# New ranks for the opening of a fused attention and feed-forward kernel, one rounding moved from GpSimd to ScalarE, and one subtraction placed beside another stage

## The chip, the cores and the metric

The kernel runs on one core of one Trainium2 chip. The metric is the device time of one execution in microseconds; a median of several runs is given. A core has five engines with queues of their own, which run in order: TensorE (PE, matrix products), VectorE (DVE), ScalarE (ACT), GpSimd (POOL), and SyncE (SP), which issues the DMA transfers here. PE reads its operands from SBUF and writes to PSUM[...].

## The reference

```python
q, k, v: (4, 4, 1088, 32);  S1, S2: (8, 32) float64;  w1, w2: (128, 1024), w3: (1024, 1024), w_out: (1024, 128) float64

def phi(x):                                   # 64 features from 32 numbers
    a = np.einsum('rd,bhsd->bhsr', S1, x)
    b = np.einsum('rd,bhsd->bhsr', S2, x)
    return np.einsum('bhsi,bhsj->bhsij', a, b).reshape(*x.shape[:-1], 64)
q_p, k_p = phi(q), phi(k)
kv = np.einsum('bhsf,bhsd->bhfd', k_p, v)
z = np.sum(k_p, axis=2)
num = np.einsum('bhsf,bhfd->bhsd', q_p, kv)
den = np.einsum('bhsf,bhf->bhs', q_p, z)[..., None] + 1e-06
x = (num / den).transpose(0, 2, 1, 3).reshape(4352, 128)
out = ((x @ w1) * (x @ w2) @ w3) @ w_out      # (4352, 128)
```

The denominator can come close to zero, so it needs more than float32's precision in the products that lead to it. The kernel gets this by splitting numbers into a leading part, rounded to a coarse grid, and a rest.

## The kernel before

**Stages.** The 4 batches of 1088 rows are cut into 9 groups: two of 512 columns for each batch (groups 0 to 7) and one of 256 columns with the remaining 64 rows of every batch (group 8). For each batch b there is a *key stage*: keys are split (`peak`, `first`, `second`), their Gram matrix is summed on PE (`gs0`, `gs1`, and `rg` for the remaining 64 rows of each batch), and a chain of small steps takes it through the sketches S1 and S2 to the matrix R, from which the denominators follow: `G_lead`, `G_rest`, `T_mm`, `T_lead`, `T_rest`, `N_mm`, `N_lead`, `N_rest`, alternately on DVE and PE. Beside it the key features `kp` are formed and summed against v (`k_ab`, `b_copy`, `kp`, `kv`, and `r_tr` to `rv` for the remaining rows). For each group there is a *query stage*: `tr` (transpose on DVE), `grid` (row maximum to a rounding constant), `lead` (two ACT instructions that give the rounded query q1), `rem` (POOL adds: the rest q2 of the query), `ay1` and `ay2` (PE products with R), `split`, `dens`, `dens2`, `phi` on DVE, then transposes and `nd` on PE and a copy that gives xT. Then the *feed-forward stage* of the group: for each of 8 chunks c `a` and `b` on PE (two products each), `a_copy` on ACT, `mul` on DVE, and `o` on PE with w3·w_out, which is formed once in the kernel (`w3_t`, `w3_t_copy`, `w3_mm`). The float64 weights come as raw words and are converted on ACT (`words`) and DVE (`conv`).

**Order.** No queue's order is written out by hand. Every step is entered into a `Plan` with an engine, an estimated duration, what it reads and writes, and a rank. `Plan.order()` simulates the five queues: for each engine it takes, among the steps that could start within 0.1 us of the earliest, the one with the lowest rank; a step of much lower rank (by over 0.9) that becomes ready within 0.35 us (`FIRST["wait"]`) is waited for. Tiles with few buffers are handed out in the order of entry. The instructions are issued in the order that results, and each engine keeps it. The steps of the opening have ranks from the table `EARLY` (-10 where it has no entry, -9 for the first query), those of the later stages from `FIRST`. `HELD` names the DVE steps that the planner takes to be slowed by POOL: 0.7 of the overlap is added to their duration.

**The opening.** `first_ops()` enters batch 0's key stage; `q_ops(0)` and `q_ops(1)` the queries of the first two groups. Groups 0 to 2 are "lean": `ay1` and `ay2` are separate steps. `first_rest` and `second_rest` split the remaining 64 rows of the keys of two batches (`kkr`): for batch 0 on POOL, with an add and a subtract of the constant for each half of the rows. Where the planner sees a gap of PE over 0.5 us before the first `o`, the kernel fills it with products on zeros (`idle`), on top of 14 of them at the very start:

```python
            if spare and t - busy > 0.5:
                idle(int((t - busy - 0.2) / 0.187))
```

The weight loads after the first two wait for a memset of one element on DVE, which is issued when the planner has passed `G_rest`.

Of the kernel before, what the change touches and what calls it, by code (L numbers as in the profile page):

```python
# [11 lines left out]
F32 = mybir.dt.float32  # L12
# [7 lines left out]
ACT = mybir.ActivationFunctionType  # L20
# [7 lines left out]
def bview(t, free):  # L28
# [12 lines left out]
MOST = 120  # L41
TURN = 0.1

FIRST = {"words": 1, "conv": 1.5, "early": 1.5, "k": 2, "KX": 10, "q": 0.8, "q_act": 1, "k_act": 0, "a": 2, "b": 2.1,
         "o": 0.9, "many": 6, "late": 3, "w3_t": 1, "w3_t_copy": 0, "w3_mm": 1.7, "k1": 1.3, "mul": 0.55, "wait": 0.35}

EARLY = {"tr": -9, "Pg": -8, "sT": -10, "grid": -8, "split": -10, "grid1": -2, "tr1": -7, "rem": -8.5, "rem1": -6,
         "lead": -10, "lead1": -6, "R": -7, "k_ab0": -11, "k_ab1": -6, "r_ab": -9, "r_tr": -9, "kv0": -12, "kv1": -5,
         "rv": -10, "P_mm": -12, "P_copy": -8, "P": -8, "kp0": -8, "kp1": -10, "r_kp": -8.5, "peak1": -8.5, "gs1": -12,
         "k_tr": -10, "rg": -11, "second_r": -9.5}  # L50

HELD = {"dens", "dens2", "conv", "second", "T_rest"}
LATENCY = {"PE": 0.27, "DVE": 0.2, "ACT": 0.23, "POOL": 0.3, "SP": 3.8}


class Plan:
# [36 lines left out]
    def order(self):  # L93
        ops = self.ops
        tiles = {tag: list(keys) for tag, keys in self.held.items()}
        end, left, res, clock = {}, [], [], {}
        columns = 128
        issued = []
        pool, held = [], (0.0, 0.0)
        turn = {}  # L100
        for op in ops:
            for key in op[5]:
                if key[0] not in SHARED:
                    turn.setdefault(key[0], []).append(key)
        for n, (_, engine, us, *_r) in enumerate(ops):
            if engine is None:
                end[n] = (None, us)
            else:
                left.append(n)

        def seen(n, engine):
            e, t = end[n]
            return t if e in (None, engine) and e != "SP" else t + LATENCY[e]

        while left:
            best = {}
            for i in left:
                _, engine, us, _, deps, new, rank = ops[i]
                if any(d not in end for d in deps):
                    continue  # L120
                t = max([clock.get(engine, 0.0)] + [seen(d, engine) for d in deps])
                ok = all(key[0] in SHARED or turn[key[0]][0] == key for key in new)
                for key in new:
                    before = tiles.get(key[0], [])
                    if len(before) >= BUFS[key[0]]:
                        users = self.users[before[-BUFS[key[0]]]]
                        if any(u not in end for u in users):
                            ok = False
                            break
                        t = max([t] + [seen(u, engine) for u in users])  # L130
                if engine == "PE" and COLUMNS.get(ops[i][0], 128) != columns:
# [22 lines left out]
            left.remove(i)  # L154
# [22 lines left out]
def kernel(  # L177
# [20 lines left out]
    nc = tc.nc  # L198
# [251 lines left out]
    def round_to(dst, src, g, engine=nc.vector):  # L450
        engine.tensor_scalar(dst, src, g, g, ALU.add, ALU.subtract)
# [237 lines left out]
    def rest_rows(m):  # L689

        for i in range(2):
            rows = slice(i * SR, (i + 1) * SR)
            yield k_rs[m][rows], kk_rs[rows, i], rows

    def first_rest(m, g, engine):
        for x, t, rows in rest_rows(m):
            if engine is nc.vector:
                round_to(t[:, 0], x, g[rows])
                continue
            gb = bview(g[rows], [[0, H], [0, D]])  # L700
            engine.tensor_add(t[:, 0], x, gb)
            engine.tensor_sub(t[:, 0], t[:, 0], gb)

    def second_rest(m, engine):
        for x, t, _ in rest_rows(m):
# [2 lines left out]
    def lead_first():  # L708

        g = {}  # L710

        def peak(n):
            g[n] = row_max(k_sb[0] if n == 0 else k_rs[0], 128, f"k{n}")

        def peaks():
            nc.vector.tensor_tensor(g[0], g[0], g[1], ALU.max)
            to_grid(g[0], 8)
            k_lead[0] = work.tile([128, 2, H, NJ, D], F32, tag="kk", bufs=1, name="kk")

        def first():  # L720
            round_to(k_lead[0][:, 0], k_sb[0], g[0])

        def second(part):
            t = k_lead[0]
            nc.vector.tensor_sub(part(t[:, 1]), part(k_sb[0]), part(t[:, 0]))
        chunks = lambda half: lambda t: t[:, :, 4 * half:4 * half + 4]
        return {"peak0": lambda: peak(0), "peak1": lambda: peak(1), "peaks": peaks,
                "first": first, "second0": lambda: second(chunks(0)), "second1": lambda: second(chunks(1)),
                "first_r": lambda: first_rest(0, g[0], nc.gpsimd), "second_r": lambda: second_rest(0, nc.gpsimd)}

    def lead(b):

# [447 lines left out]
    def q_ops(g):  # L1180
# [21 lines left out]
                p.op("load", "SP", 1.6, lambda: load_by_head("q", b + 2), (), (("qh", b + 2),), 3)  # L1202
        op("grid", "DVE", 0.35 + 0.6 * w, (qT,), (("gq", g),), after=begin)
        op("lead", "ACT", 0.2 + 1.2 * w, (qT, ("gq", g)), (("q1", g), ("q2", g)))
        op("rem", "POOL", 1.15, (qT, ("q1", g), ("q2", g)), (("q2", g),))
        R = [*(("R", b) for b in batches), *(("Rs", n) for n in range(4))]
        if lean:
            op("ay1", "PE", 0.25, (("q1", g), *(R if g else (("Rh", 0), ("Rs", 0)))), (("wa", "ay", g),), after=last_phi)
# [119 lines left out]
    def first_ops():  # L1328
# [19 lines left out]
        op("first", "DVE", 0.73, "first", (("k", 0), ("gk", 0)), (("kk", 0),))  # L1348
        op("second0", "DVE", 0.62, "second0", (("k", 0), ("kk", 0)), (("k2", 0),))
        op("second1", "DVE", 0.65, "second1", (("k", 0), ("kk", 0)), (("k2", 1),))  # L1350
        op("first_r", "POOL", 1.7, "first_r", (("kr", 0), ("gk", 0)), (("kkr", 0),))
        op("second_r", "POOL", 0.95, "second_r", (("kr", 0), ("kkr", 0)), (("kkr", 0),))
# [20 lines left out]
        op("P", "POOL", 1.93, sketch_P, (("Pc",), ("Pg",)), (("P",),))  # L1373
        op("T_lead", "DVE", 0.9, "T_lead", (("t", "T"),), (("Tp", 0),))
# [99 lines left out]
```

## Time and profile before

| what | us |
|---|---|
| median of 13 runs (276.28 to 278.57) | 277.52 |
| the profiled execution, its own time | 277.34 |
| its span, first to last instruction | 275.3 |
| PE busy (share of the span) | 268.2 (97%) |
| DVE busy | 209.1 (76%) |
| ACT busy | 122.7 (45%) |
| POOL busy | 21.3 (8%) |
| products on zeros, L358: 55 instructions | 14.8 |

The profile is of one execution. Its timeline gives for each row the start in us from the span's start, the duration, engine, line, operation, out <- in with the shape, and in brackets the idle time before it with what ended it. Rows of the same kind that follow one another are merged, with their count. A second view gives busy time by stretch of the span, a third the chain of work that ended last. Busy PE time holds the products on zeros too. The granted clock of PE is 1.000 of full speed in the mean.

### The profile page before, as it was taken

What the parts mean: (1) busy time and instruction counts of PE and PEld (TensorE: products, weight loads), DVE (VectorE), ACT (ScalarE), POOL (GpSimd) and SP (SyncE); (2) the same over time, 40 slices, a digit from 0 to 9 for tenths busy, and PEclk for the clock granted to TensorE, in tenths of its full rate; (3) what the DMA queues carried; (4) which work ended last, traced back from release to release, by engine and by line L of the source; (5) the groups of instructions that cost most, each with busy time, mean ns of one, the idle gap of its engine ahead of it and who ended that gap; (6) DMA issues with size and microseconds to landing.
All of it is one profiled execution on the core that took longest, in us unless ns stands there. A gap on an engine that the chain in (4) does not pass through costs nothing.

```text
span 275.3 us, 6300 instructions
## 1 busy us (share of the span) xinstructions
PE 268.2 (97%) x2556; PEld 150.8 (55%) x2556; DVE 209.1 (76%) x507; ACT 122.7 (45%) x265; POOL 21.3 (8%) x31
## 2 busy tenths in 40 slices
PE   7989999999999999999999999999999999999995
PEld 3766544477774767745544446455544544444665
DVE  7889999999999999996648699847695585583231
ACT  4693796997775992111332240224123222323120
POOL 2772000100000010000010010001000100000000
PEclk9999999999999999999999999999999999999999
DMA  4739999579930220020200200020002002000203
GB/s 128 280 93 298 256 381 271 157 206 291 257 120 2 76 85 2 2 39 2 38 2 0 37 4 5 0 39 2 0 0 41 0 2 38 2 0 10 31 0 57
DMA packets 28876, 22.42 MB, mean 81 GB/s; under 512 B 20016, under 2 KB 25392, under 8 KB 28848
## 3 DMA queue, kind: packets, MB, share of 16 engines
q1 hardware_dynamic: 28704, 21.96, 29.2%
q8 instruction: 20, 0.33, 0.5%
q14 instruction: 8, 0.07, 0.1%
q10 hardware_dynamic: 144, 0.07, 0.1%
HBM read 19.80 MB, written 2.23 MB: 80 GB/s over the span
## 4 chain that ended last, share of the span: by engine, by line
PE 89%; DVE 7%; ACT 2%; issue 1%; DVEq 0%; ACTq 0%
PE ps_o L1292 21%; PE b_ps L1273 20%; PE a_ps L1263 20%; PE ps_w3o L577 5%; PE ps_kvz L775 4%; PE ps_wt L565 3%; PE idle_ps L358 3%; PE ps_c L1034 2%; PE ps_o L1288 1%; PE ps_xt L1156 1%; PE ps_ab L672 1%; DVE ab L1278 1%; DVE ph L1109 1%; PE ps_c L1047 1%; PE ps_c L1045 1%
## 5 line engine op out<-in xcount | busy, mean ns | idle before, releaser
L1268 ACT COPY ffa<-a_ps 128x512 f32<-128x512 f32 (+1 forms) x72 | 40.4, 562 | 104.1 <-PE a_ps L1263 103.4
L1278 DVE TENSOR_TENSOR ab<-ffa,b_ps 128x512 f32<-128x512 f32 (+1 forms) x72 | 46.6, 650 | 41.1 <-PE b_ps L1273 38.3
L1273 PE MATMUL b_ps<-xT,w 128*128 128x512 f32 (+1 forms) x144 | 71.1, 575 | 0.0
L1263 PE MATMUL a_ps<-xT,w 128*128 128x512 f32 (+1 forms) x144 | 70.6, 572 | 0.1
L1292 PE MATMUL ps_o<-ab,w3o 128*128 128x512 f32 x128 | 65.7, 605 | 0.0
L1273 PEld LDWEIGHTS b_ps<-xT,w 128*128 128x128 f32 x144 | 26.2, 190 | 29.1 <-issue 24.3
L1263 PEld LDWEIGHTS a_ps<-xT,w 128*128 128x128 f32 x144 | 26.3, 190 | 27.2 <-issue 19.8
L1292 PEld LDWEIGHTS ps_o<-ab,w3o 128*128 128x128 f32 x128 | 22.8, 190 | 21.3 <-issue 18.8
L1007 POOL TENSOR_TENSOR q<-qT,q 128x512 f32<-128x512 f32 x8 | 9.6, 1196 | 184.1 <-ACT q L1003 180.6
L375 ACT CAST sgn<-cv_c 128x512 f16<-128x512 f32 x22 | 17.0, 773 | 0.0
L358 PE MATMUL idle_ps<-zeros 128*128 128x448 bf16 x55 | 14.8, 418 | 1.8 <-DVE zeros L352 1.8
L577 PE MATMUL ps_w3o<-wo,w3T 128*128 128x128 f32 x128 | 15.8, 275 | 0.5 <-issue 0.5
L577 PEld LDWEIGHTS ps_w3o<-wo,w3T 128*128 128x128 f32 x128 | 15.1, 192 | 1.1 <-issue 0.8
L411 ACT ACTIVATE cv_c<-raw 128x512 f32<-128x512 f32 x22 | 15.2, 689 | 0.0
L414 ACT ACTIVATE cv_m<-raw 128x512 int32<-128x512 uint32 x22 | 15.0, 682 | 0.0
L424 DVE CUSTOM_DVE_ANT_0 w3c<-w3c,cv_m 128x1024 uint16<-128x1024 uint16 x16 | 11.9, 742 | 0.4
L1109 DVE TENSOR_TENSOR ph<-ay,bs 128x512 f32<-128x512 f32 (+1 forms) x12 | 11.1, 947 | 0.2
L421 DVE SCALAR_TENSOR_TENSOR w3c<-cv_c,sgn 128x512 int32<-128x512 int32 x16 | 10.9, 684 | 0.3 <-ACT sgn L375 0.3
L565 PEld LDWEIGHTS ps_wt<-ident,w3c 128*128 128x128 f32 x64 | 7.7, 144 | 6.0 <-issue 2.8
L358 PEld LDWEIGHTS <-zeros 128*128 128x128 bf16 x55 | 5.9, 113 | 8.2 <-issue 3.8
L572 ACT COPY w3T<-ps_wt 128x512 f32<-128x512 f32 x16 | 9.4, 588 | 2.1 <-PE ps_wt L565 1.8
L565 PE MATMUL ps_wt<-ident,w3c 128*128 128x128 f32 x64 | 9.8, 276 | 0.0
(213 smaller groups left out, 355.1 us busy)
## 6 DMA issues: line engine op xcount, KB each, us to landing
raw<-in_moe_w_dram SPq DMA_DIRECT2D x20, 512.0 KB, 6.4
qh<-in_q_dram SPq DMA_DIRECT2D x4, 544.0 KB, 7.1
out_dram<-oT SPq DMA_DIRECT2D x33, 64.0 KB, 2.0
k_sb<-in_k_dram SPq DMA_DIRECT2D x4, 512.0 KB, 9.4
kh<-in_k_dram SPq DMA_DIRECT2D x12, 128.0 KB, 3.8
v_sb<-in_v_dram SPq DMA_DIRECT2D x12, 128.0 KB, 7.0
raw<-in_moe_w_out_dram SPq DMA_DIRECT2D x2, 512.0 KB, 6.8
v_sb<-in_v_dram SPq DMA_DIRECT2D x1, 512.0 KB, 5.3
```

The costliest lines, as they stand in the source:

```text
L358: nc.tensor.matmul(ps[:, :448], zeros[:, :128], zeros, start=True, stop=True)
L375: nc.scalar.copy(bview(t.bitcast(F16)[:, 1:], [[2, n]]), c)
L411: nc.scalar.mul(x["c"], halves(raw[n], CW)[1].bitcast(F32), 2.0 ** -112)
L414: nc.scalar.mul(x["m"].bitcast(I32), halves(raw.pop(n), CW)[0].bitcast(U32), 2.0 ** -29)
L565: nc.tensor.transpose(ps[i][:, c], w3c[i][:, c * 128:(c + 1) * 128], ident)
L577: nc.tensor.matmul(ps["mm"], w3T[ko][:, c], wo[:, c], start=(c == 0), stop=(c == NC - 1))
L1109: nc.vector.tensor_mul(ph[:, j:j + step].rearrange("p j h a b -> p (j h) a b"), bview(a, [[r, step * H], [1, r], [0, r]]), bview(b, [[r, s ...
L1263: nc.tensor.matmul(a_sb[g, c, "ps"][:, :n], w1[:, c * 128:(c + 1) * 128], xT[key], start=True, stop=True)
L1268: nc.scalar.copy(a_sb[g, c][:, :n], a_sb.pop((g, c, "ps"))[:, :n])
L1273: nc.tensor.matmul(ab_sb[g, c, "ps"][:, :n], w2[:, c * 128:(c + 1) * 128], xT[key], start=True, stop=True)
L1278: nc.vector.tensor_mul(ab_sb[g, c][:, :n], a_sb.pop((g, c))[:, :n], ab_sb.pop((g, c, "ps"))[:, :n])
L1292: nc.tensor.matmul(o_ps[g][:, :n], w3o[:, c], ab_sb.pop((g, c))[:, :n], start=c == 0, stop=c == NC - 1)
```

## The change

It has three parts.

1. `first_rest` for batch 0 runs on ACT: a `[128,1]` product by -1 that gives the negative constant, and then for each half of the rows one activation with the constant as bias, and one with its negative. `second_rest` stays on POOL.
2. In group 1, `rem` is entered behind `ay1` and depends on it; before it followed `lead`.
3. The tables change: `EARLY` gets new ranks for most steps of the opening (the Gram products, `P_mm`, `k_tr` and `first_r` have the lowest; `k_ab`, `kp`, `kv` and the remaining keys' steps the highest), `FIRST` has other ranks for `b`, `o` and `w3_t_copy`, `HELD` has three more names, and some estimated durations differ. The planner's search keeps a set of the steps whose inputs are planned, with the same rule of choice.

```diff
-FIRST = {..., "k_act": 0, "a": 2, "b": 2.1,
-         "o": 0.9, "many": 6, "late": 3, "w3_t": 1, "w3_t_copy": 0, "w3_mm": 1.7, ...}
-EARLY = {"tr": -9, "Pg": -8, "sT": -10, "grid": -8, "split": -10, "grid1": -2, "tr1": -7, "rem": -8.5, "rem1": -6,
-         "lead": -10, "lead1": -6, "R": -7, "k_ab0": -11, "k_ab1": -6, "r_ab": -9, "r_tr": -9, "kv0": -12, "kv1": -5,
-         "rv": -10, "P_mm": -12, "P_copy": -8, "P": -8, "kp0": -8, "kp1": -10, "r_kp": -8.5, "peak1": -8.5, "gs1": -12,
-         "k_tr": -10, "rg": -11, "second_r": -9.5}
-HELD = {"dens", "dens2", "conv", "second", "T_rest"}
+FIRST = {..., "k_act": 0, "a": 2, "b": 1.9,
+         "o": 1.95, "many": 6, "late": 3, "w3_t": 1, "w3_t_copy": 0.3, "w3_mm": 1.7, ...}
+EARLY = {"first_r": -13, "k_tr_copy": -12.5, "tr": -9, "Pg": -9.5, "sT": -9.2, "grid": -8, "split": -10, "grid1": -7,
+         "tr1": -7.5, "rem": -11, "rem1": -4.5, "lead": -11, "lead1": -8, "R": -7, "k_ab0": -6, "k_ab1": -5.9, "r_ab": -5.5,
+         "r_tr": -5.6, "kv0": -5, "kv1": -5, "rv": -5, "P_mm": -12, "P_copy": -9.5, "P": -12, "kp0": -5, "kp1": -5,
+         "r_kp": -4.6, "peak1": -9.5, "gs1": -12, "k_tr": -12, "rg": -11.5, "second_r": -12, "gs0": -12, "b_copy": -9,
+         "ay2": -10, "ay1": -11}
+HELD = {"dens", "dens2", "conv", "second", "T_rest", "phi", "second0", "second1"}
...
     def first_rest(m, g, engine):
+        if engine is nc.scalar:
+            minus = work.tile([128, 1], F32, tag="g_minus", bufs=1, name="g_minus")
+            engine.mul(minus, g, -1.0)
+            for grid, first in ((g, True), (minus, False)):
+                for x, t, rows in rest_rows(m):
+                    engine.activation(t[:, 0], x if first else t[:, 0], ACT.Identity, bias=grid[rows])
+            return
         for x, t, rows in rest_rows(m):
-            if engine is nc.vector:
-                round_to(t[:, 0], x, g[rows])
-                continue
-            gb = bview(g[rows], [[0, H], [0, D]])
-            engine.tensor_add(t[:, 0], x, gb)
-            engine.tensor_sub(t[:, 0], t[:, 0], gb)
+            round_to(t[:, 0], x, g[rows])
...
-                "first_r": lambda: first_rest(0, g[0], nc.gpsimd), ...
+                "first_r": lambda: first_rest(0, g[0], nc.scalar), ...
...
-        op("rem", "POOL", 1.15, (qT, ("q1", g), ("q2", g)), (("q2", g),))
+        def rem(after=()):
+            op("rem", "POOL", 1.15, (qT, ("q1", g), ("q2", g)), (("q2", g),), after=after)
+        if g != 1:
+            rem()
...
-            op("ay1", "PE", 0.25, ...)
+            ay1 = op("ay1", "PE", 0.25, ...)
+            if g == 1:
+                rem((ay1,))
...
-        op("first_r", "POOL", 1.7, "first_r", (("kr", 0), ("gk", 0)), (("kkr", 0),))
-        op("second_r", "POOL", 0.95, ...)
+        op("first_r", "ACT", 1.3, "first_r", (("kr", 0), ("gk", 0)), (("kkr", 0),))
+        op("second_r", "POOL", 1.0, ...)
-        op("P", "POOL", 1.93, ...)
-        op("T_lead", "DVE", 0.9, ...)
+        op("P", "POOL", 1.95, ...)
+        op("T_lead", "DVE", 0.7, ...)
```

More of the change, by code (lines that the diff above doesn't have):

```diff
@@ L42 @@
 TURN = 0.1
-FIRST = {"words": 1, "conv": 1.5, "early": 1.5, "k": 2, "KX": 10, "q": 0.8, "q_act": 1, "k_act": 0, "a": 2, "b": 2.1,
-         "o": 0.9, "many": 6, "late": 3, "w3_t": 1, "w3_t_copy": 0, "w3_mm": 1.7, "k1": 1.3, "mul": 0.55, "wait": 0.35}
-EARLY = {"tr": -9, "Pg": -8, "sT": -10, "grid": -8, "split": -10, "grid1": -2, "tr1": -7, "rem": -8.5, "rem1": -6,
-         "lead": -10, "lead1": -6, "R": -7, "k_ab0": -11, "k_ab1": -6, "r_ab": -9, "r_tr": -9, "kv0": -12, "kv1": -5,
-         "rv": -10, "P_mm": -12, "P_copy": -8, "P": -8, "kp0": -8, "kp1": -10, "r_kp": -8.5, "peak1": -8.5, "gs1": -12,
-         "k_tr": -10, "rg": -11, "second_r": -9.5}
-HELD = {"dens", "dens2", "conv", "second", "T_rest"}
+FIRST = {"words": 1, "conv": 1.5, "early": 1.5, "k": 2, "KX": 10, "q": 0.8, "q_act": 1, "k_act": 0, "a": 2, "b": 1.9,
+         "o": 1.95, "many": 6, "late": 3, "w3_t": 1, "w3_t_copy": 0.3, "w3_mm": 1.7, "k1": 1.3, "mul": 0.55, "wait": 0.35}
+EARLY = {"first_r": -13, "k_tr_copy": -12.5, "tr": -9, "Pg": -9.5, "sT": -9.2, "grid": -8, "split": -10, "grid1": -7,
[4 rows of a table added]
+HELD = {"dens", "dens2", "conv", "second", "T_rest", "phi", "second0", "second1"}
 LATENCY = {"PE": 0.27, "DVE": 0.2, "ACT": 0.23, "POOL": 0.3, "SP": 3.8}
@@ L113, in seen @@
             return t if e in (None, engine) and e != "SP" else t + LATENCY[e]
-        while left:
+        behind, open_deps, ready = {}, {}, set()
+        for n in left:
+            deps = [d for d in ops[n][4] if d not in end]
+            open_deps[n] = len(deps)
+            if not deps:
+                ready.add(n)
+            for d in deps:
+                behind.setdefault(d, []).append(n)
+        while ready:
             best = {}
-            for i in left:
+            for i in ready:
                 _, engine, us, _, deps, new, rank = ops[i]
-                if any(d not in end for d in deps):
-                    continue
                 t = max([clock.get(engine, 0.0)] + [seen(d, engine) for d in deps])
@@ L153, in order @@
             t, i, engine = first
-            left.remove(i)
+            ready.remove(i)
+            for n in behind.get(i, ()):
+                open_deps[n] -= 1
+                if not open_deps[n]:
+                    ready.add(n)
             us = ops[i][2]
@@ L695, in first_rest @@
     def first_rest(m, g, engine):
-        for x, t, rows in rest_rows(m):
-            if engine is nc.vector:
-                round_to(t[:, 0], x, g[rows])
-                continue
-            gb = bview(g[rows], [[0, H], [0, D]])
-            engine.tensor_add(t[:, 0], x, gb)
-            engine.tensor_sub(t[:, 0], t[:, 0], gb)
+        if engine is nc.scalar:
[5 more added lines that the diff above has]
+            return
+        for x, t, rows in rest_rows(m):
+            round_to(t[:, 0], x, g[rows])
     def second_rest(m, engine):
@@ L728, in lead_first @@
                 "first": first, "second0": lambda: second(chunks(0)), "second1": lambda: second(chunks(1)),
-                "first_r": lambda: first_rest(0, g[0], nc.gpsimd), "second_r": lambda: second_rest(0, nc.gpsimd)}
+                "first_r": lambda: first_rest(0, g[0], nc.scalar), "second_r": lambda: second_rest(0, nc.gpsimd)}
     def lead(b):
@@ L1204, in q_ops @@
         op("lead", "ACT", 0.2 + 1.2 * w, (qT, ("gq", g)), (("q1", g), ("q2", g)))
-        op("rem", "POOL", 1.15, (qT, ("q1", g), ("q2", g)), (("q2", g),))
+        def rem(after=()):
+            op("rem", "POOL", 1.15, (qT, ("q1", g), ("q2", g)), (("q2", g),), after=after)
+        if g != 1:
+            rem()
         R = [*(("R", b) for b in batches), *(("Rs", n) for n in range(4))]
         if lean:
-            op("ay1", "PE", 0.25, (("q1", g), *(R if g else (("Rh", 0), ("Rs", 0)))), (("wa", "ay", g),), after=last_phi)
+            ay1 = op("ay1", "PE", 0.25, (("q1", g), *(R if g else (("Rh", 0), ("Rs", 0)))), (("wa", "ay", g),), after=last_phi)
+            if g == 1:
+                rem((ay1,))
         else:
@@ L1350, in first_ops @@
         op("second1", "DVE", 0.65, "second1", (("k", 0), ("kk", 0)), (("k2", 1),))
-        op("first_r", "POOL", 1.7, "first_r", (("kr", 0), ("gk", 0)), (("kkr", 0),))
-        op("second_r", "POOL", 0.95, "second_r", (("kr", 0), ("kkr", 0)), (("kkr", 0),))
+        op("first_r", "ACT", 1.3, "first_r", (("kr", 0), ("gk", 0)), (("kkr", 0),))
+        op("second_r", "POOL", 1.0, "second_r", (("kr", 0), ("kkr", 0)), (("kkr", 0),))
         for half in range(2):
@@ L1372, in first_ops @@
         op("Pg", "DVE", 0.58, sketch_P_peak, (("Pc",),), (("Pg",),))
-        op("P", "POOL", 1.93, sketch_P, (("Pc",), ("Pg",)), (("P",),))
-        op("T_lead", "DVE", 0.9, "T_lead", (("t", "T"),), (("Tp", 0),))
+        op("P", "POOL", 1.95, sketch_P, (("Pc",), ("Pg",)), (("P",),))
+        op("T_lead", "DVE", 0.7, "T_lead", (("t", "T"),), (("Tp", 0),))
         op("T_rest", "DVE", 0.55, "T_rest", (("t", "T"), ("Tp", 0)), (("Tb", 0),))
```

## Prediction

> **What bounds the kernel now.** I read the busy tenths first, then the timelines of the engines from 6 to 36 us, then the busy times by stretch.
>
> ```profile
> PE   7989999999999999999999999999999999999995
> DVE  7889999999999999996648699847695585583231
> ```
>
> From the fifth slice on TensorE (PE) is full. By stretch it is busy 10.00 of 10 us in every one from 70 to 130 us, and between 33.6 and 70 it lacks 0.6 us. VectorE (DVE) is full too, until about 118 us. So the feed-forward part is work that PE does without gaps; only an earlier start of it, or less work left at that start, moves the end. What sets the start is one chain in the first 34 us, mostly on DVE, with the rest of PE's time filled by products on zeros. The timeline of DVE, and that of PE's first product and first feed-forward product:
>
> ```profile
> 1.81 6.12 PE L358 MATMUL idle_ps<-zeros 128*128 128x448 bf16 x16 [1.81 <-DVE zeros L352]
> 8.98 0.19 DVE L519 COPY ST<-ps_s 128x32 f32<-128x32 f32 x1 [0.94 <-PE ps_s L516]
> 9.47 1.02 DVE L451 TENSOR_SCALAR kk<-k_sb,g_k 128x1024 f32<-128x1024 f32 x1
> 10.52 1.69 DVE L725 TENSOR_TENSOR kk<-k_sb,kk 128x512 f32<-128x512 f32 x2
> 14.17 0.18 DVE L440 TENSOR_REDUCE g_pair<-ps_kvz 128x1 f32<-128x32 f32 x1
> 15.76 0.41 DVE L834 TENSOR_TENSOR gB<-gb,mask 128x128 f32<-128x128 f32 x1
> 18.35 0.90 DVE L464 TENSOR_TENSOR Ts<-Ta,Tb 128x8 f32<-128x8 f32 x1
> 27.04 1.74 DVE L1109 TENSOR_TENSOR ph<-ay,bs 128x512 f32<-128x512 f32 x2
> 41.99 1.29 DVE L1109 TENSOR_TENSOR ph<-ay,bs 128x512 f32<-128x512 f32 x2
> 33.62 1.02 PE L1263 MATMUL a_ps<-xT,w 128*128 128x512 f32 x2
> ```
>
> And POOL (GpSimd) beside it:
>
> ```profile
> 10.01 1.65 POOL L706 TENSOR_TENSOR kkr<-k_sb,kkr 64x128 f32<-64x128 f32 x2
> 11.95 2.08 POOL L656 TENSOR_TENSOR kp<-b_sb 128x1024 f32<-128x1024 f32 x1 [0.28 <-ACT b_sb L648]
> 16.16 1.96 POOL L656 TENSOR_TENSOR kp<-b_sb 128x1024 f32<-128x1024 f32 x1
> 18.07 1.16 POOL L1007 TENSOR_TENSOR q<-qT,q 128x512 f32<-128x512 f32 x1
> 26.47 1.16 POOL L1007 TENSOR_TENSOR q<-qT,q 128x512 f32<-128x512 f32 x1 [3.46 <-DVE rc L1096]
> ```
>
> The reader should see pairs. Ts has 8 elements and takes 0.90 us, ending at 19.25 where POOL's 18.07 + 1.16 ends; its neighbours of that size take 0.17. The first ph waits for 26.47 + 1.16 and the pair takes 1.74 instead of 1.29.
>
> **What the Trainium skill says.** "SBUF — State Buffer", section "Who interferes with whom": a DVE instruction with two SBUF inputs, or in a two-port mode, and a GpSimd instruction that reads SBUF exclude each other for a whole instruction, and the first to issue wins. The pairs above agree, to 0.05 us. DVE operations that read PSUM ran beside kp undisturbed (17.06 to 18.3). "TensorE: Matmul & The Clock Gate", Part 1: the array starts at half clock. The trace agrees: 16 early fillers take 0.38 us each, 11 at 16.88 take 0.20.
>
> So DVE loses in the opening: 0.94 waiting for ps_s, 0.2 in `first` (1.02; the same form alone takes 0.81), 0.45 in `second` (two 0.62 alone), 0.12 in gB, 0.73 in Ts, 0.45 in phi: 2.9 us in all.
>
> **The change part by part.** The ranks only alter the order in which each engine issues; I worked that order out by hand from the planner's rules, and take times from the trace. Rewriting the planner's loop, and the new duration entries, cost nothing on the chip by themselves.
>
> 1. *sT after first and second.* DVE no longer waits for ps_s. `first` runs 8.05 to 8.80, `second` to 10.1, where it ended at 12.21.
>
> 2. *first_r on ScalarE (ACT).* Five instructions replace four of POOL's (4 x 0.39). No row of before has this shape. "ScalarE: Activation LUTs", section "What ACT_TABLE_LOAD costs", gives 280 + 0.833 N ns with a pointer bias and 93 ns overlap; L1002 at N=512 takes 720 where that gives 707. Estimate for N=128: 4 x 0.29 + 0.19 = 1.35 us; lower bound 1.0, at the 0.21 spacing of L526. I take 1.35. In ACT's order P_copy precedes it, which waits for PE to 8.96, so it ends at 10.3, and second_r on POOL (2 x 0.39, now after `second`) at about 11.3. Its reader rg needs it at 12.1: covered by 0.8 us. Behind it on ACT are the two kT copies, 0.7 us late (to 11.4); their reader k_ab0 now comes after rg, so the Gram products cover this. Uncovered it would cost 0.7.
>
> 3. *PE: Gram products before k_ab.* The transposes leave PE at 9.74; the planner now sees a gap of 1.1 us there and puts about four fillers in (0.75 us). gs0 starts at 10.5 and not at 9.74; gs0 to rg took 2.0 with one wait of 0.1, so rg ends at 12.43 (before 13.41). The query's grid, which stood ahead of G_lead, comes later. G_lead starts at 12.45 instead of 14.17: **1.7 us gained so far**.
>
> 4. *But kp0 and kp1 now meet the G and T chains.* k_ab0 follows rg: 0.87, two ACT copies 0.43, 0.14 to POOL: kp0 starts 1.5 us after rg and holds the port 1.96. gB starts 1.6 us after rg. Kp0 wins by 0.1, and gB ends at about 16.05 (before 16.17). Then the query's grid (1.05) runs on DVE, T_lead at 17.1, Ts at 18.4 after kp1 (16.05 to 18.0): Ts ends 18.55. If gB wins, it ends at 14.3, but kp1 then runs 16.25 to 18.2 and Ts, due at 16.7, ends at 18.3. Either way **0.7 to 0.95 remains** of the 1.7.
>
> 5. *N chain.* tr for group 1 (0.83) now lies before N_lead, as grid for group 1 (0.98) did. N_lead starts at 19.4 (before 20.15).
>
> 6. *Split, dens, phi.* rem of group 1 waits for its ay1 and leaves phi alone: 0.45 gained. But the remaining keys' r_tr now follows ay2, so r_kp (0.63) falls into dens, whose operations read SBUF twice: up to 0.6 lost, 0 if it falls between PSUM readers; I take 0.4. Phi ends at 28.0 (before 28.78).
>
> 7. *Group 1's grid* (1.02) is still to do. Then the four conversions of w1 and w2 (2.65): they end at 31.65, before 31.4. The copy to xT waits for group 1's two activations on ACT (1.45). So the first a starts at about 31.5, before 33.62, but ay2 of group 1 (1.9 us of PE) comes after it and not before. PE gains 2.1 - 1.9 = 0.2 us; DVE is 0.2 behind.
>
> 8. *Feed-forward ranks* (b 1.9, o 1.95, w3_t_copy 0.3). The h tiles are handed out in a fixed order, so b cannot pass an a; b and w3's products now pass o. The same PE work, with PE full: nothing. There is 1.1 us of filler and gap after 33.6 to gain at most 0.5 from; a worse fit to DVE could open new gaps, and I bound this at 1.5 lost.
>
> 9. *SP's queue.* Its gate is DVE's one-element memset (16.86), now behind the query's grid: about 17.1. What waits are raw 2 and 3, used near 41 us, so the 0.2 is hidden; if their slack were gone, it would be 0.2.
>
> Sum, in the profiled execution (277.34, 275.3 span + 2.04 around it): -0.2, so 277.1. That execution lies 0.18 below the median of 13; I forecast **277.2 us**, no change that can be told (0.3%, 0.83 us, is about what a measurement of this kernel can tell).
>
> **Rivals.**
> - *The port is dodged.* If gB wins and T_lead comes before the grid, Ts waits at kp0's end and goes in before kp1. Then only about 0.6 of the 2.9 us remains lost, and 2.0 to 2.3 is gained: 275.2. For it: kp0's margin is 0.1. Against: the grid is ready a whole T_mm before T_lead.
> - *kp1 lands on the N chain.* If b_copy of half 1 stands behind group 0's lead on ACT (18.6 at the end), kp1 runs 18.75 to 20.7 and rem to 21.9: Rh waits 0.4, Rf and Rl up to 1.1, and ay2 waits for q2, so dens begins 1.3 to 1.7 later than in my sum: 278.7. It decides as soon as kp1 starts after 18.4. For it: lead outranks b_copy (-11, -9). Against: b_copy is ready some 1 us earlier.
> - *It does not do what it says*: first_r waits on ACT behind P_copy, second_r is then hit by DVE as before, and the fillers take the rest: 277.5.
>
> **How the numbers follow.** Forecast 0.40 (its own range 276.4 to 277.9; 0.32 same, 0.04 either way); port dodged 0.28; kp1 on the N chain, or a worse fit in step 8, 0.27; not what it says 0.05, same. Faster 0.32, same 0.37, slower 0.31. The range 274.9 to 279.6 takes in both rivals, with 0.3 below the first, and 0.9 above the second for part of step 8's bound.
>
> **What would show it.** Right: `first` starts at 8.05 with no wait for ps_s; G_lead near 12.5; gB or Ts over 1 us long, ending with a kp; ph pair 1.29; first a near 31.5 with ay2 of group 1 after it. Wrong: T and N chains 2 us earlier without a stretched operation, kp1 after 18.4, or new PE gaps between 34 and 110 us.

## The result, and the profile after

The changed kernel is slower: a median of 279.89 us (278.93 to 281.04) against 276.77 us for the kernel before on the same chip. The ratio is 1.0108, with a 95% interval of 1.0088 to 1.0128: 3.0 us (2.4 to 3.5). The profiled execution took 280.85 us, with a span of 279.1.

The busy tenths of the changed kernel, one digit for each fortieth of the span (about 7 us), with TensorE's granted clock:

```profile
PE   7989999999999989999999999999999999999995
DVE  7966999999999999995638868866785488383231
...
PEclk9955999999999999999999999999999999999999
```

The same clock row of the kernel before:

```profile
PEclk9999999999999999999999999999999999999999
```

Two digits of PEclk are new. In the third and fourth slice, 14 to 28 us, PE ran at half speed. DVE's third and fourth digits fall with it, from 8 and 9 to 6 and 6. And PE's row has an 8 in the fifteenth slice, near 102 us, where before it had a 9. These two places are where I looked for the loss. Within the executions of the changed kernel the time goes with the mean granted clock: 278.93 us at 1.000 (one of the 12 on record), 279.05 to 279.39 at 0.994, 280.76 to 281.04 at 0.976 and 0.982. The kernel before loses clock too, but seldom: 28 of its 143 later executions are below 0.999, most of them at 0.992 to 0.994.

The timeline of DVE in the opening (start, duration, engine, line, operation, and in brackets the idle time before with what ended it):

```profile
7.94 0.81 DVE L463 TENSOR_SCALAR kk<-k_sb,g_k 128x1024 f32<-128x1024 f32 x1
8.79 1.58 DVE L739 TENSOR_TENSOR kk<-k_sb,kk 128x512 f32<-128x512 f32 x2
...
11.75 0.15 DVE L452 TENSOR_REDUCE g_pair<-ps_kvz 128x1 f32<-128x32 f32 x1
...
13.43 1.83 DVE L848 TENSOR_TENSOR gB<-gb,mask 128x128 f32<-128x128 f32 x1
...
17.45 0.17 DVE L476 TENSOR_TENSOR Ts<-Ta,Tb 128x8 f32<-128x8 f32 x1
...
20.40 0.17 DVE L452 TENSOR_REDUCE g_pair<-ps_N 128x1 f32<-128x8 f32 x1 [2.04 <-PE ps_N L484]
...
29.17 1.29 DVE L1123 TENSOR_TENSOR ph<-ay,bs 128x512 f32<-128x512 f32 x2
```

What the change was meant to do is there. `first` starts as soon as its constant is ready, with no wait for ps_s. G_lead (the row at 11.75) starts 2.4 us earlier than in the profile before; part of that is this execution and not the change, since its first 16 products on zeros took 4.48 us, against 6.12 in the profile before (in warm below, 5.70, with G_lead at 12.15). Ts takes 0.17 and not 0.90, the phi pair 1.29 and not 1.74. But gB takes 1.83 us (undisturbed it takes 0.29, as kp_wait shows below), and at 20.40 DVE has waited 2.04 us for N_mm. The timelines of GpSimd and of ScalarE show why gB is long, and what first_r costs there:

```profile
13.16 3.91 POOL L668 TENSOR_TENSOR kp<-b_sb 128x1024 f32<-128x1024 f32 x2 [0.23 <-ACT b_sb L660]
```

```profile
8.05 0.81 ACT L713 ACTIVATE kkr<-k_sb,g_k 64x128 f32<-64x128 f32 x2
8.88 0.82 ACT L713 ACTIVATE kkr<-kkr,g_minus 64x128 f32<-64x128 f32 x2
```

kp0 began 0.27 us ahead of gB, and gB ended at 15.26, just behind kp0. In that time PE had nothing to do. The timeline of PE, with its two waits after the opening:

```profile
15.31 0.60 PE L484 MATMUL ps_T<-ST,gB 128*128 128x8 f32 x2 [1.42 <-DVE gB L848]
15.77 3.52 PE L370 MATMUL idle_ps<-zeros 128*128 128x448 bf16 x9
...
20.30 1.94 PE L789 MATMUL ps_kv<-kp,v_sb 128*32 128x64 f32 x64
...
34.76 1.02 PE L1283 MATMUL a_ps<-xT,w 128*128 128x512 f32 x2
...
103.21 0.63 PE L577 MATMUL ps_wt<-ident,w3c 128*128 128x128 f32 x4 [0.82 <-DVE w3c L436]
...
113.83 2.05 PE L589 MATMUL ps_w3o<-wo,w3T 128*128 128x128 f32 x16 [0.35 <-DVE ay_C L1072]
```

And the same stretch by windows (busy us of PE, PEld, DVE, ACT, POOL with their counts; the third number from the end is the granted clock):

```profile
14.00:15.00 1.00, 0.00 (x0) 0.00 (x0) 1.00 (x1) 0.25 (x2) 1.00 (x1) 0.84 0.00 0
15.00:22.00 7.00, 6.68 (x81) 4.83 (x81) 4.50 (x23) 5.70 (x12) 3.23 (x3) 0.50 0.61 154
22.00:28.00 6.00, 6.00 (x39) 4.92 (x29) 3.84 (x12) 0.66 (x4) 0.25 (x1) 0.50 1.08 340
28.00:29.00 1.00, 1.00 (x6) 0.48 (x5) 0.90 (x4) 0.00 (x0) 0.37 (x1) 0.83 0.99 216
```

PE is empty in the whole of the microsecond from 14 to 15, and within it the clock falls to 0.50. A mean of 0.84 says that it fell at 14.68 (0.68 of the us at 1.0, the rest at 0.5); a mean of 0.83 from 28 to 29 says that it rose at 28.34. These 13.7 us hold nine fillers (products on zeros) of 0.39 us each, both N_mm, the kv sums (1.94 us for 64 products, 1.10 at full clock, in warm) and all of ay2. So the first a comes at 34.76, later than the 33.62 of the profile before, though the Gram chain started earlier.

### The profile page after: what moved, and what is told of

It reads as the page before. It is cut to its first block, busy times and chain, and to the rows that moved or that the text cites. A ratio compares the mean times of both kernels' runs of the same rounds, so it can differ in the third digit from the quotient of the medians.

```text
span 279.1 us, 6294 instructions
## 1 busy us (share of the span) xinstructions
PE 271.3 (97%) x2552; PEld 153.7 (55%) x2552; DVE 209.2 (75%) x507; ACT 125.0 (45%) x270; POOL 19.9 (7%) x27
## 4 chain that ended last, share of the span: by engine, by line
PE 86%; DVE 11%; issue 1%; ACT 0%; DVEq 0%; ACTq 0%
PE b_ps L1293 21%; PE a_ps L1283 21%; PE ps_o L1312 20%; PE ps_w3o L589 3%; PE idle_ps L370 3%; PE ps_kvz L789 2%; PE ps_wt L577 2%; PE ps_c L1048 2%; PE ps_c L1061 1%; PE ps_o L1308 1%; PE ps_xt L1170 1%; PE ps_ab L684 1%; PE ps_c L1059 1%; DVE w3c L433 1%; PE ps_x L1144 1%
## 5 line engine op out<-in xcount | busy, mean ns | idle before, releaser
L1312 PE MATMUL ps_o<-ab,w3o 128*128 128x512 f32 x128 | 63.6, 605 | 0.0
L1293 PEld LDWEIGHTS b_ps<-xT,w 128*128 128x128 f32 x144 | 26.6, 190 | 27.5 <-issue 24.8
L1021 POOL TENSOR_TENSOR q<-qT,q 128x512 f32<-128x512 f32 x8 | 10.2, 1278 | 183.8 <-ACT q L1017 116.4
L436 DVE CUSTOM_DVE_ANT_0 w3c<-w3c,cv_m 128x1024 uint16<-128x1024 uint16 x16 | 11.0, 690 | 0.4
```

The source lines that it names most:

```text
L1293: nc.tensor.matmul(ab_sb[g, c, "ps"][:, :n], w2[:, c * 128:(c + 1) * 128], xT[key], start=True, stop=True)
L1312: nc.tensor.matmul(o_ps[g][:, :n], w3o[:, c], ab_sb.pop((g, c))[:, :n], start=c == 0, stop=c == NC - 1)
```

## Experiments

The theory after the first look was: (1) gB meets kp0, PE runs dry, the clock falls, and this is about half of the loss; (2) the rest is a worse fit of the feed-forward part to DVE, or something that the moved query leaves behind.

**warm**: the changed kernel, with PE kept busy.

```diff
-        step()
+        step(), idle(8 * (name == "T_mm1"))
```

> The changed kernel, its order untouched, with eight more products on zeros put on TensorE between T_mm1 and T_mm2, where the profile after shows 1.4 us without work just before the granted clock falls to 0.50. Clock theory (that hole drops the clock, and the half clock from 15 to 28 us is a main part of the loss): granted clock 1.000, N_lead starts near 18.4 instead of 20.4, and the time is that of the changed kernel's run with a full clock, 278.9, so 1.0 below the changed kernel's median of 279.9. Rank theory (the loss is in the feed-forward part, the clock is a by-thing): no change, 279.9. Prediction's theory (only the SBUF port costs, in the G and T chains): no change, 279.9.

278.22 us, ratio 1.0054 (1.0037 to 1.0072). Its timeline of PE:

```profile
14.26 1.67 PE L370 MATMUL idle_ps<-zeros 128*128 128x448 bf16 x8
15.81 0.39 PE L484 MATMUL ps_T<-ST,gB 128*128 128x8 f32 x2
...
18.80 1.10 PE L789 MATMUL ps_kv<-kp,v_sb 128*32 128x64 f32 x64
...
31.31 1.02 PE L1283 MATMUL a_ps<-xT,w 128*128 128x512 f32 x2
...
100.78 0.63 PE L577 MATMUL ps_wt<-ident,w3c 128*128 128x128 f32 x4 [0.82 <-DVE w3c L436]
...
111.40 2.05 PE L589 MATMUL ps_w3o<-wo,w3T 128*128 128x128 f32 x16 [0.35 <-DVE ay_C L1072]
```

gB is as long as before (2.01 us), so nothing of the lock itself is taken away, only PE's empty time. The clock stays at 0.999 or more in all 22 executions, the first a comes at 31.31, and the time falls by 1.7 us by the medians (the kernel before had 276.77 beside the one and 276.33 beside the other), or from 1.0108 to 1.0054, which is 1.5 us. The time is 0.7 us lower than the expectation had it. About half of the loss is the clock. The two waits near 101 and 111 us stay, to the hundredth.

**before_hole**: the suspected cost alone, put into the kernel before. The edit leaves out the eleven products on zeros ahead of the first N_mm, which stand in the profile before as

```profile
16.88 2.24 PE L358 MATMUL idle_ps<-zeros 128*128 128x448 bf16 x11
18.96 0.28 PE L470 MATMUL ps_N<-Ta,P 128*128 128x8 f32 x2
```

```diff
-            if spare and t - busy > 0.5:
+            if spare and t - busy > 0.5 and name != "N_mm1":
```

> The kernel before without the 11 products on zeros ahead of its first N_mm, so that PE has nothing to do for some 2 us near 17 to 19 us. It leaves out no computation. If a hole of this size lets the granted clock fall, as is read from the changed kernel: 0.50 for one or more stretches of 3.4 us from about 19 us on, ay2 and the later products of the opening at half speed, and 278 to 279.5. If the clock was lost for another reason: within 0.3% of before.

278.86 us, ratio 1.0069 (1.0040 to 1.0098). Timeline of PE, then windows:

```profile
17.26 0.36 PE L470 MATMUL ps_N<-Ta,P 128*128 128x8 f32 x2 [1.44 <-DVE Tb L462]
```

```profile
18.00:19.00 1.00, 1.00 (x34) 0.98 (x34) 0.90 (x5) 1.00 (x3) 0.89 (x1) 0.59 0.92 254
19.00:21.00 2.00, 2.00 (x21) 1.16 (x14) 1.33 (x9) 0.23 (x1) 0.00 (x0) 0.50 0.84 247
21.00:22.00 1.00, 1.00 (x9) 1.00 (x8) 0.90 (x4) 0.27 (x2) 0.38 (x1) 0.71 1.00 301
```

A hole of 1.44 us brings the clock down at 18.18 and up again at 21.58 (worked out as above): 3.40 us at half speed. Confirmed: a hole of this size was enough, in the other kernel and at another place. This is the shortest and fastest case: the profiled execution took 277.15 us at a mean clock of 0.992. All nine were below the full clock, and four of them, at 0.975, took 279.15 to 279.89. What decides how long the half clock lasts is not shown.

**kp_G and kp_wait**: kp0 behind gB. In kp_G the two kp were entered behind G_rest, with a dependency on it.

```diff
-            op(f"kp{half}", "POOL", 1.92, ..., (("w3c", "b", half),), ...)
+            op(f"kp{half}", "POOL", 1.92, ..., (("w3c", "b", half), ("Gb", 0)), ...)   # behind G_rest
```

> The changed kernel with both kp of batch 0 made to wait for G_rest, so that GpSimd cannot hold the port when gB comes; VectorE's order is the same. Port theory: gB takes 0.3 instead of 1.83, T_mm2 ends near 14.3, TensorE has no hole there and the clock stays at 1.000; Ts, due near 16, then meets a kp and ends at about 17.8, N_lead at about 18.7: 278.9 or a little less. Rank theory: 279.9. If the half clock has another cause than the hole: gB short, clock below 1.000, about 279.9.

279.87 us, ratio 1.0117 (1.0076 to 1.0157), a failed experiment: kp0 still started at 13.67, 0.10 us ahead of gB, which took 2.00. A dependency in this plan orders the issue; on the chip the instruction didn't wait, as it touches no data of gB. kp_wait makes it touch gB:

```diff
+            def kp0_late(kp=st["kp0"]):
+                z = work.tile([128, 1], F32, tag="z_wait", bufs=1, name="z_wait")
+                nc.gpsimd.tensor_copy(z, acc["G"][1][:, :1])
+                kp()
+            st["kp0"] = kp0_late
```

> The changed kernel with one copy of a single column of gB to GpSimd's queue ahead of the first kp, so that kp0 cannot start before gB has ended (no extra products on zeros). If the lock of gB by kp0 made the hole in PE that let the clock fall: gB takes 0.3 instead of 1.83 us, T_mm2 follows near 14 instead of 15.3, the granted clock stays at 1.0 to 36 us, Ts may wait for kp0's end near 16, the first a comes near 31, and the time is 277.4 to 278.3 as with the extra fillers. If the clock falls for another reason (few products in the whole stretch from 12 to 20 us): first a 34 to 35 and 279.5 to 280 again.

279.15 us, ratio 1.0090 (1.0063 to 1.0116). Timelines of DVE, GpSimd and PE:

```profile
13.87 0.29 DVE L854 TENSOR_TENSOR gB<-gb,mask 128x128 f32<-128x128 f32 x1
...
16.35 1.90 DVE L476 TENSOR_TENSOR Ts<-Ta,Tb 128x8 f32<-128x8 f32 x1
```

```profile
14.36 3.86 POOL L668 TENSOR_TENSOR kp<-b_sb 128x1024 f32<-128x1024 f32 x2
```

```profile
18.39 0.36 PE L484 MATMUL ps_N<-Ts,P 128*128 128x8 f32 x2 [1.35 <-DVE Ts L476]
```

gB is short again, and T_mm2 starts at 14.38. But kp1 follows kp0 without a gap, Ts loses to it and ends at 18.25, as the prediction's fourth step said for the case that gB wins. PE's hole has only moved, from gB to Ts (1.35 us), and the clock fell once more, at 20.82. So the expectation failed: it had the clock at 1.0 and 277.4 to 278.3 us. That gB was long because of kp0 is shown (0.29 for 2.00). That the clock falls for one hole, and not for too little work in the whole stretch from 12 to 20 us, is not shown by this run, since it has both.

**kp_both**: kp1 held behind Ts as well, in the same way.

> The changed kernel with kp0 held behind gB and kp1 held behind Ts, each by a one-column copy on GpSimd. Neither gB nor Ts meets a kp: gB 0.29, Ts 0.17 us near 16.4, N_mm2 follows at once. If the hole that one kp makes in PE is what lets the clock fall, it now stays at 1.0, N_lead comes near 17.7 (18.9 in the one with extra fillers), first a near 30.5, and the time is 277.2 to 278.2; it does not come below before if DVE's later work and the feed-forward order take what is gained. If the clock falls all the same: 279 to 280.

278.82 us, ratio 1.0086 (1.0055 to 1.0116). Timelines of DVE and PE:

```profile
16.36 0.17 DVE L476 TENSOR_TENSOR Ts<-Ta,Tb 128x8 f32<-128x8 f32 x1
...
18.45 1.52 DVE L900 TENSOR_TENSOR Rh<-Na,mask4n 128x32 bf16<-128x32 f32 x1
```

```profile
20.02 0.28 PE L1042 MATMUL ps_a<-Rh,q 128*128 128x64 bf16 x4 [1.25 <-DVE Rh L900]
```

Now kp1 meets Rh, the next DVE operation with two SBUF operands, and PE has its hole of 1.25 us there. Here half of the executions kept a mean clock of 0.994 or more, and they took 277.9 to 278.1 us: no better than warm. So holding both kp back gains nothing against warm; in kp_wait and kp_both each kp that was moved met the next such operation of the chain (Ts, then Rh).

**act_only**: the first part of the change alone, at a fixed place in the order of before (first_r behind the two copies of the transposed keys).

> The kernel before with only the first part of the change: first_r on ScalarE, set behind the two copies of the transposed keys, second_r behind it on GpSimd; every other step in the order of before. By my working `first` takes 0.81 and each `second` 0.62 (0.65 us less on DVE), but second_r ends near 13.3, so rg ends up to 0.4 later, and b_copy 0 on ScalarE is 1.7 us later, which brings kp0 to gB. Within 0.3% of before, 276.0 to 277.6. If the kp0 that is moved there makes a hole in PE as in the changed kernel: 278 or more.

280.49 us, ratio 1.0162 (1.0126 to 1.0198), the worst of all. `second` ran undisturbed (1.29 for two), but kp0 came at 13.04, as the expectation feared, and PE waited for kp0 itself:

```profile
15.05 0.65 PE L782 MATMUL ps_kv<-kp,v_sb 128*32 128x64 f32 x32 [1.54 <-POOL kp L656]
```

A hole of 1.54 us, and half speed from 16.62 to 20.04. In the profiled execution another part of the time is 1.8 us at the very end, told in the last section.

**newfirst and oldfirst**: the feed-forward ranks alone. newfirst is the kernel before with the new values of `b`, `o` and `w3_t_copy`, oldfirst the changed kernel with the old ones.

> The kernel before with only the ranks of b, o and w3_t_copy of the change (1.9, 1.95, 0.3). Rank theory: 1.2 us slower than before, 278.0, with a gap of TensorE near 100 to 115 us. Clock theory and port theory: same as before, 276.8, clock 1.000.

> The changed kernel with the ranks of b, o and w3_t_copy of before (2.1, 0.9, 0); the opening keeps the changed ranks. Rank theory (the new ranks leave TensorE waiting for VectorE between 100 and 114 us, 1.2 us in the profile after): 278.7, no wait of w3_mm for ay_C. Clock theory: the opening is the same, so the clock still drops in most runs and the time is 279.9. If both hold: 278.7 with a clock below 1.000.

newfirst: 277.05 us, ratio 1.0006 (0.9988 to 1.0025). oldfirst: 279.55 us, ratio 1.0101 (1.0066 to 1.0135). The new ranks by themselves cost nothing that can be measured, and the old ones repair nothing. In oldfirst the two waits above are gone, but four others, 1.14 us in all, take their place.

**new_tail and old_tail**: the two openings, each with the other's order from planned time 31 us on. The order was written out as a list of steps.

```diff
-    for t, n in p.order():
+    plan, tail = p.order(), [int(x) for x in TAIL.split()]
+    head = [x for x in plan if x[0] < 31.0]
+    for t, n in head + [(None, n) for n in tail]:
```

> The kernel before until planned time 31 us, and from there every step in the order in which the changed kernel issues it. Theory A, the order of the feed-forward part costs it: 278.0 or more, with 5 to 6 us of waits of PE between 80 and 118 us. Theory B or C, the opening decides: within 0.3% of before, 276 to 277.

> The opening of the changed kernel with its eight extra products on zeros (so PE's clock stays up), and from planned time 31 us on every step in the order in which the kernel before issues it, with that kernel's three later fillers. Theory A, the order of the feed-forward part costs the 1.9 us that remained with the clock up: the waits of PE between 80 and 118 us fall from 5.8 to about 3.4 us, as in the kernel before, and the time is 275.8 to 276.5. Theory B, DVE is the second full engine until 118 us and had gained nothing in the opening, so PE's earlier start must come back as waits whatever the order: 276.3 to 277.0, the same as before. Theory C, the opening itself leaves something behind (the second group's query, later loads): 278.2 as with the changed order.

new_tail, the kernel before with the changed order of the later part: 277.54 us, ratio 1.0050 (1.0031 to 1.0070), 1.4 us: between what the two theories had forecast (278.0 or more, and 276 to 277). Its timeline of PE has the two waits of the changed kernel:

```profile
99.37 0.63 PE L596 MATMUL ps_wt<-ident,w3c 128*128 128x128 f32 x4 [0.81 <-DVE w3c L455]
...
110.00 2.05 PE L608 MATMUL ps_w3o<-wo,w3T 128*128 128x128 f32 x16 [0.37 <-DVE ay_C L1089]
```

They are in every kernel that issues the later part in the changed order (after, warm, kp_G, kp_wait, kp_both and this one: 0.81 or 0.82, and 0.35 to 0.37), and in none of the others. So the later order costs something in the opening of before too, as theory A said, but 1.4 us and not the 1.9 of its forecast. old_tail took 279.42 us, ratio 1.0099 (1.0073 to 1.0126), which no theory had expected. In its profiled execution 1.8 us is a last DMA issue of 2.20 us (last section). If all its executions have that, some 277.6 remains, 0.7 us above the median of before (276.85), with a new wait of 1.26 us at 67.6 us. An order planned for one opening doesn't fit the other, so this half of the pair separates nothing.

**rem1**: the second part of the change alone, with the tables of before.

> The kernel before with only the second part of the change: rem of group 1 entered behind its ay1. By my working phi's pair takes 1.29 instead of 1.74 us, everything on DVE behind it comes 0.45 earlier, first a near 33.2, ay2 of group 1 after it: 276.0 to 276.8. Rival, the second group's late ay2 delays its dens and with it DVE's feed-forward products: 277.3 to 278, slower by 0.3 to 0.5%.

277.52 us, ratio 1.0027 (1.0005 to 1.0048). The time is that of the expectation's rival (277.3 to 278), but its reason is not seen: ay2 of group 1 does come late, at 31.83, and yet den of group 1 starts at 38.63, against 39.25 in before_short. Where the 0.05 to 0.48% go stays open. The expectation failed in its first point: the phi pair took 1.74 as before, and rem stood beside it, at 24.99. The new dependency on ay1 is of the kind seen in kp_G. It moves rem in the order of issue; rem reads nothing of ay1, and q1 was ready. In the changed kernel it is the late grid and lead of group 1 that keep rem away from phi.

**before_short**: the kernel before with `idle(10)` for `idle(14)` at the very start.

> The kernel before with 10 instead of 14 products on zeros at the very start. In its profiled execution these ran at half clock to 7.9 us, and sT on DVE waited 0.94 us for ps_s, which the first step of the prediction counts as a gain; in other executions of it the span is 273.7 to 274.3 at full clock, and not 275 to 275.8. Theory A, the wait for ps_s is there only when the clock of the start comes late: with four fillers less it is gone in all executions, sT follows the constants at once near 8.0, and the median is 275.8 to 276.3, like the lower half of before. Theory B, the two levels of before have another cause: the median stays within 0.1% of before, with both levels.

276.16 us, ratio 0.9984 (0.9968 to 1.0000), the lowest median here, below both kernels, at the edge of what can be told. Timelines of DVE and PE:

```profile
7.82 0.18 DVE L519 COPY ST<-ps_s 128x32 f32<-128x32 f32 x1
...
25.55 1.75 DVE L1109 TENSOR_TENSOR ph<-ay,bs 128x512 f32<-128x512 f32 x2
```

```profile
32.15 1.02 PE L1263 MATMUL a_ps<-xT,w 128*128 128x512 f32 x2
```

sT follows the constants with no wait, and the first a comes at 32.15, 1.5 us ahead of the profile that the prediction was made from. The kernel before, too, often runs so: 69 of 115 of its executions at full clock have spans of 273.7 to 274.6, and the profiled one had 275.3. "Gone in all executions" was too much: 5 of 22 here still lie near 275.3, with a cause that I did not find.

**warm_q1b**: warm, with rem of group 1 directly behind lead again, and ranks that put grid and lead of group 1 ahead of N_lead.

> The changed kernel with the eight extra products on zeros, and with the second group's query put back beside the first: rem directly behind lead as before, and ranks for grid and lead of group 1 that bring them ahead of N_lead, so that ay2 of group 1 comes before the first a again. Theory A, the late query of group 1 is what changes the order of the feed-forward part and so makes PE wait for w3c and for ay_C between 99 and 113 us (1.2 us in every run with the changed order): these two waits are gone, and the time is 276.3 to 277.2. Theory B, the waits come from the opening itself or from the new ranks of the feed-forward part: they stay, and the time is 278 or more. GpSimd's rem meets DVE's operations again, so up to 0.5 us may be lost near 24 us.

278.70 us, ratio 1.0072 (1.0049 to 1.0096). The two waits near 100 and 111 us are gone, as theory A said, so the place of the second query does shape the later order. But the time did not fall, and so neither theory's forecast came true in full. In 7 of the 21 executions the mean clock was 0.994, and they took 279.69 to 280.84 us; the other 14 have a median of 278.05. Another wait has taken the place of the two on PE, larger than both together:

```profile
67.59 0.63 PE L577 MATMUL ps_wt<-ident,w3c 128*128 128x128 f32 x4 [2.13 <-DVE gb L858]
```

The windows around it, in the same execution, keep the full clock (PE is busy for 0.46 and 0.00 us; the third number from the end is the clock):

```profile
65.00:66.00 1.00, 0.46 (x34) 0.29 (x23) 0.96 (x2) 1.00 (x3) 0.00 (x0) 1.00 1.01 387
66.00:67.00 1.00, 0.00 (x0) 0.00 (x0) 0.90 (x5) 0.74 (x2) 0.00 (x0) 1.00 1.04 362
```

And the first a, with ay2 of group 1 done, comes at 33.10. In warm it comes at 31.31 with 1.76 us of ay2 still due, the same within 0.03. Beside the 32.15 of before_short, with ay2 done, the changed opening is 0.9 us behind, though its clock is up. This compares one execution of each.

## Why the prediction was wrong

The forecast was 277.2 us; with the clock held up the changed kernel takes 278.22, and as it stands 279.89. Two terms were missing, and a third was measured against the wrong execution.

**Steps 1 to 4, the opening: right in mechanism.** `first` without a wait, fillers of 0.92 us ahead of the Gram products, G_lead earlier, kp0 ahead of gB by a little (I had said 0.1 us, it was 0.27), gB to the end of kp0, T_lead behind the query's grid, Ts behind kp1 and undisturbed. first_r on ScalarE was priced too low: four activations took 1.63 us and the product 0.20, against 1.35 in all. The duration from the Trainium skill's page "ScalarE: Activation LUTs", section "What ACT_TABLE_LOAD costs", agrees (0.387 by the page, 0.385 to 0.402 here); the overlap of 0.093 that I took off each was not there. It was covered all the same: second_r ended at 10.69, and its reader rg started at 11.14. But second_r did not come after `second`: it began at 9.37, beside it, and in this execution `second` took 1.58 us where warm has 1.29.

**The step that failed first is step 4**, in what it left out. It let gB wait for kp0 and asked only when gB would end. It did not ask what PE does meanwhile. The planner does not know of the lock, so it puts no fillers there; PE stood empty for 1.42 us, and the clock fell for 13.7 us. The cost that the prediction put at nothing is this one. I had quoted the skill's page "TensorE: Matmul & The Clock Gate", Part 1, for the start alone. Its section "HAM oscillation — how this bites in real kernels" warns of idle gaps above about 3.4 us, so by its figure a hole of 1.4 us would be harmless. Here it was not: in the profiled executions of seven kernels a hole of 1.25 to 1.54 us was followed by the half clock (after, oldfirst, kp_G, kp_wait, kp_both, before_hole, act_only). The measurement decides. The length of a hole is not the whole rule either: the 2.13 us in warm_q1b left the clock at 1.00, as did a hole of 1.26 us in old_tail at 67.6 us. The window of 3413 ns that Part 1 of the page gives does agree: half speed, worked out from the windows as above, lasted 3.40 us in before_hole, 3.42 in act_only, 6.8 in kp_wait and in kp_both, and 13.7 in the changed kernel, which is one, one, two, two and four such windows. Cost: 1.5 us by the ratios of the changed kernel and warm, 1.7 by their medians.

**Steps 5 to 7 were right at full clock.** warm has N_lead at 18.91 (I had 19.4), a port loss of 0.44 in `pr` (I had 0.4), phi's pair at 1.29 with its end at 27.5 (28.0), and the first a at 31.31 (31.5), with ay2 of group 1 behind it. One reason was wrong: I credited phi's 0.45 us to rem's dependency on ay1, and rem1 shows that the dependency holds nothing.

**The step that failed second is step 8**, sized at nothing with 1.5 lost as its bound. I argued that PE's work is the same and PE is full. But from 30 to 118 us DVE is as full as PE, as I had written myself in the first part, and an order that is planned anew meets DVE's results at other times. Two waits of 0.82 and 0.35 us came of it, 1.4 us (0.9 to 1.9) by new_tail, inside the bound that I had given and then left out of the sum. Nor was it the ranks that I had looked at (newfirst: none). The opening's planned times changed, and with them the planner's later order.

**The gain of step 1** was real against the profiled execution of before, but that is not the typical one. The wait of 0.94 us for ps_s is missing in before_short and, by their spans, in about 6 of 10 executions of the kernel before. Its median in later runs was 276.3 to 277.2 us, and not the 277.52 that I forecast from. Against an opening without that wait (before_short) the changed one loses 0.9 us and does not gain 0.2.

The sum: 1.0108 for the change; 0.54% less with the clock up; 0.50% for the later order put into the kernel before. Together these are 1.04%. The opening itself, with its clock up, is then worth about nothing on the mean of executions. This takes the parts as adding up, and by the intervals of the three ratios it is good to some 0.3% (an estimate).

**The rivals.** "kp1 lands on the N chain" did not happen by itself; kp_both brought it about. "The port is dodged" was worth 2.0 to 2.3 us in my working; with kp0 and kp1 held back kp_both is no better than warm, since a third operation is hit. A run in which no operation of the chain is hit was not made, so its worth stays open. A worse fit in step 8 was rival enough to be named, and was the part of the third case that came true. No case held a lower clock, and so the range ended 0.3 us below the result.

**What stays open:** which single place of the second query would give both a good opening and a later order without waits, and what the second level of before_short is. Open too is why the clock falls in some executions of a kernel and not in others.

## What to carry to other kernels

When a step is stretched by a lock or a wait, look at the engine behind it as well: if that engine is TensorE, and the planner hasn't filled the hole, the price can be not the hole but a half clock that follows. Where a planner orders everything, an edit early in the program changes the order of all that comes later, so run the two halves crossed before blaming either. And forecast from an execution whose level is typical: a stall that one profile shows may be missing from more than half of the runs.

## What had not been expected of the hardware

Holes of 1.25 to 1.54 us in PE's work were followed by the half clock in seven profiled executions, all in the opening, where the products around them are mostly small (8 columns in T_mm and N_mm, 64 in the kv sums). The fall came within the hole (the changed kernel: 14.68) or up to 2.4 us after its end (before_hole: end 17.26, fall 18.18; act_only: 15.05 and 16.62; kp_wait: 18.39 and 20.82). A longer hole elsewhere was not: the 2.13 us of warm_q1b come behind kv sums of 64 columns and ahead of products of 128, and left the clock at 1.00. So did the waits of 0.82 and 0.35 us later on, and, in the opening of the profile before, a hole of 0.87 us that ended at 15.84. No run here separates the length of a hole from the size of the products around it, or from the moment at which it falls.

The last of the output transfers is issued from ScalarE's queue and not from SyncE's. In old_tail this issue took 2.20 us, in the kernel before 0.37. The timelines of old_tail and of the kernel before (ACTq is ScalarE's queue):

```profile
273.52 2.20 ACTq L1375 DMA_DIRECT2D out_dram<-oT  x1
```

```profile
272.76 0.37 ACTq L1324 DMA_DIRECT2D out_dram<-oT  x1
```

act_only has it too (2.19 us); the thirteen other profiles don't. It adds 1.8 us to the span of these two executions, in a way that no theory of the order explains, and its cause was not tried. Whether the other executions have it is not known.
